# A mixture-of-experts kernel: the second expert's first weights split earlier, the third expert's rows turned later, one set of small loads moved back

## The chip, the cores and the metric

The kernel runs on one core of a Trainium2 chip. Its five engines work from instruction streams of their own: TensorE (PE, with its weight loads shown apart as PEld), VectorE (DVE), ScalarE (ACT), GpSimd (POOL) and SyncE (SP), which here issues nearly all loads. The metric is the device time of one execution in microseconds (us), median of the runs. Before the change it is 405.98 us (3 runs, 405.19 to 406.72).

## The reference

Two parts, one feeding the other. The first is a recurrent attention over 4 batches, 8 heads, 768 steps and 48 channels per head; the second is a mixture of 8 experts over its 3072 rows of 384 columns, where each row goes to the one expert with the highest logit:

```
y[:, :, t] = einsum('bhd,bhde->bhe', rt, state + u*kt (x) vt)
state      = wt * state + kt (x) vt
logits = x @ w_gate;  expert_idx = argmax(logits);  gate_w = softmax(logits)[expert_idx]
for e in range(8):                       # rows sorted by expert
    h = maximum(x_sorted[lo:hi] @ w1[e], 0.0)      # 384 -> 1024
    y_sorted[lo:hi] = h @ w2[e]                    # 1024 -> 384
out = gate_w[:, None] * y_sorted[inv_perm]
```

Everything is float32, and the experts' products must keep float32's accuracy.

## The kernel before

The attention part and the routing take the first 186 us; the routed rows are scattered into a DRAM buffer `xs`, each expert having a region, with two extra columns, the gate weight and the row's number (the "tag"). What the change touches is the part behind it, the function `moe`, which runs the eight experts one after the other, e = 0 to 7 (e is the place in this order; e = 1 is "the second expert").

**Splitting.** TensorE multiplies in a reduced float32 format, so each operand is split in two: a high part H, written by ScalarE (`ACT.Copy` into the reduced type), and a low part L = value - H, written by VectorE. A product is three matmuls: H by H, H by L and L by H. What is split: the weights of an expert in four groups (g = 0 and 1 the halves of w1, g = 2 and 3 the halves of w2; `W[e][2](g)`, lines 1076 and 1078, results `w1H`, `w1L`, `w2H`, `w2L`), the rows (`xsplit`, lines 1247 and 1248, `xH` and `xL`, in three column pieces c = 0 to 2), and the hidden layer (`hH`, line 1282, and `hL`, line 1283).

**One expert on TensorE.** `mm1(e, f)` for f = 0 to 7 makes 128 of the 1024 hidden columns each, nine matmuls into one of four PSUM banks in turn (`ps`, `pt`, `pp`, `pw`), which hH and hL then read. So mm1 of f + 4 needs the bank that hL of f frees. Then the second product, for d = 0 to 2, 24 matmuls each (three for every f), into the banks `pk` and `py`: `mm2` (turned: the result has the 384 output columns on partitions, and `yturn` turns it back by VectorE) for experts with more than 384 places for rows, `mm2d` for the first expert, with 256, and the last ones. The second expert has 464 columns of rows.

**Order of the work.** All is issued in the order in which the code is written (`tc.manual_schedule()`): each engine works through its own list in that order, and waits by semaphores for what others write. So where `xturn`, `xsplit` and the weight splits stand among the `mm1` calls sets what ScalarE and VectorE do between the hidden columns. Two tables say where the next expert's rows are turned and split: `turn(e, t)` is called after each f (t = f) and after each d (t = 8 + d), and does `xturn` (line 1240, one VectorE transposition of the gathered rows `xg` into `xT`) where the first number of the tuple stands and the three `xsplit` where the others do:

```
XF = ((7,7,8,8),(2,3,4,5))
for j, at in enumerate(XF[e > 0]):
    if at == t:
        if j: xsplit(e + 1, j - 1)
        else: xturn(e + 1)
```

**Loads.** SP issues, per expert and in this order: weight halves into four staging buffers `wstage` (line 1057; a buffer is free when its former group has been split), zeros behind the next expert's rows (line 1107), the gathered rows `xg` of the next expert (line 1230, one buffer, rows of 384 B) and the tags (line 1217, elements of 8 B). A DMA that touches `xs` waits for the ones before it that wrote there.

Of the kernel before, what the change touches and what calls it, by code (L numbers as in the profile page):

```python
# [27 lines left out]
FILL = ((0, 0, 0, 0), 0, 2, 0, 1, 5, 8, 0, 0, (99, 99, 20, 0), (0, 2, 0, 0), (0, 0, 0, 0))  # L28
TAIL = (1, 1, 1, 1)
XV = (1, 3)  # L30
XF = ((7,7,8,8),(2,3,4,5))
EA = (4, 5, 6, 7)
TP = 2
PULSE = (3, 2, 1)
# [12 lines left out]
def wkv_moe(ctx: ExitStack, tc: tile.TileContext, r, k, v, w, u, w_gate, w1, w2, out):  # L47
# [21 lines left out]
    NR = NT + TOPB * TB + P  # L69
# [964 lines left out]
    def turned(e):  # L1034
        return CAPS[e - 1] > 3 * P if e else (CAP - EARLY) % P > 0
# [55 lines left out]
    W = {0: weights(0)}  # L1091
    X = {}
# [5 lines left out]
    def following(e):  # L1098
        at = {}
        for nm, t, lo, hi in (("src", perm, 1, E - 1), ("end", ends, NR, E * NR - 4 * zp - P)):  # L1100
            at[nm] = nc.values_load(t[0:1, e:e + 1], engines=(mybir.EngineType.SP,), min_val=lo, max_val=hi)
        X["src", e + 1] = at["src"]
        W[e + 1] = weights(e + 1, at["src"])
        return at["end"]

    def zero_rows(end):
        nc.sync.dma_start(xs[ds(end, 4 * zp)].rearrange("(q p) x -> p q x", p=zp),
                          zrow[:zp, None, :].to_broadcast([zp, 4, ROW]))
# [88 lines left out]
    def moe():  # L1197
        with ExitStack() as a:
# [4 lines left out]
            def span(e):  # L1203
                return (EARLY, CAP) if e == 0 else (0, CAPS[e - 1])

            def blocks(e):
                lo, hi = span(e)
                return [(q, min(P, hi - q)) for q in range(lo, hi, P)]

            def tags(e, at):  # L1210
                lo, hi = span(e)
                n = hi - lo
                tag = X["tag", e] = tp.tile([P, TOPB, 2], F32, name="tag")
                if turned(e):
                    nq = -(-n // TB)
                    for g in range(P // TB):
                        nc.sync.dma_start(tag[g * TB:(g + 1) * TB, :nq], xs[ds(at, nq * TB), DM:DM + 2]
                                          .rearrange("(q t) x -> t q x", t=TB))
                    return
                nf = n // P  # L1220
                nc.sync.dma_start(tag[:, :nf], xs[ds(at, nf * P), DM:DM + 2].rearrange("(q t) x -> t q x", t=P))
                if n % P:
                    nc.sync.dma_start(tag[:n % P, nf], xs[ds(at + nf * P, n % P), DM:DM + 2])

            def xload_(e, src):
                n = CAPS[e - 1]
                nq = -(-n // TB)
                xg = X["g", e] = rp.tile([P, TOPB, XG], F32, name="xg")[:, :nq]
                for g in range(P // TB):
                    nc.sync.dma_start(xg[g * TB:(g + 1) * TB], xs[ds(src * NR, nq * TB), g * XG:(g + 1) * XG]  # L1230
                                      .rearrange("(q t) x -> t q x", t=TB))
# [5 lines left out]
            def xturn(e):  # L1237
                xg = X["g", e]
                X["T", e] = rp.tile([P, TOPB, XG], F32, name="xT")[:, :xg.shape[1]]
                nc.vector.transpose(X["T", e].rearrange("p q (c t) -> p q c t", c=KD),  # L1240
                                    xg.rearrange("p q (t c) -> p q c t", c=KD))
                xalloc(e)

            def xsplit(e, c):
                src = X["T", e][:, :, c * TB:(c + 1) * TB]
                hh, ll = (X[nm, e][:, c, :src.shape[1] * TB].rearrange("p (q t) -> p q t", t=TB) for nm in "HL")
                nc.scalar.activation(hh, src, AF.Copy)
                nc.vector.tensor_tensor(ll, src, hh.bitcast(F32), op=OP.subtract)
# [19 lines left out]
            def mm1(e, f):  # L1268
                ws = W[e][0]
                lo, hi = span(e)  # L1270
                n = hi - lo
                p = bank(("ps", "pt", "pp", "pw")[f % 4])[:, :n]
                sl = slice(f * P, (f + 1) * P)
                terms = [(c, x, y) for c in range(KD) for x, y in ("HH", "HL", "LH")]
                if f == 0:
                    terms.sort(key=lambda t: t[2] == "L")
                for j, (c, x, y) in enumerate(terms):
                    nc.tensor.matmul(p, ws["1" + x][:, c, sl], X[y, e][:, c, :n],  # L1278
                                     start=(j == 0), stop=(j == len(terms) - 1))
                hh = hp.tile([P, TOP], F32R, name=f"hH{f}")[:, :n]  # L1280
                hl = hp.tile([P, TOP], F32R, name=f"hL{f}")[:, :n]
                nc.scalar.activation(hh, p, AF.Relu)
                nc.vector.scalar_tensor_tensor(hl, p, 0.0, hh.bitcast(F32), op0=OP.max, op1=OP.subtract)  # L1283
                X["h", e, f] = (hh, hl)
# [47 lines left out]
            def yscat(e, q):  # L1332
                nc.gpsimd.memset(spacer, 0.0)
                d = nc.gpsimd.indirect_dma_start(  # L1334
                    out=out.rearrange("n (g x) -> (n g) x", g=XP),
                    out_offset=bass.IndirectOffsetOnAxis(ap=X["i", e][:, q:q + 1], axis=0),
                    in_=X["o", e][:, q], in_offset=None, bounds_check=XP * NT - 1, oob_is_err=False)
                for s in oscat:
                    tc.declare_no_dep(d.ins, s.ins, reason="every token has a row of its own")
                oscat.append(d)  # L1340
# [15 lines left out]
                otail(o, n, tag[:, 1:2])  # L1356

            def turn(e, t):
                for j, at in enumerate(XF[e > 0]):
                    if at == t:  # L1360
                        if j:
                            xsplit(e + 1, j - 1)
                        else:
                            xturn(e + 1)
# [8 lines left out]
            for e in range(E):  # L1373
                nx = e + 1 < E
                if nx:
                    if e == 0:
                        tags(0, EARLY)
                        zero_rows(res["end"])
                    elif e > 1:
                        zero_rows(following(e))  # L1380
                    W[e + 1][3](wres)
                    if e:
                        xload_(e + 1, X["src", e + 1])
                        tags(e + 1, X["src", e + 1] * NR)
                        for g in range(4):
                            W[e + 1][1](g)
                    else:
                        W[1][1](0)
                        xload_(1, X["src", 1])
                        W[1][1](1)  # L1390
                        zero_rows(following(1))
                        W[1][1](2)
                        W[1][1](3)
                        tags(1, X["src", 1] * NR)
                for f in range(KF):
                    mm1(e, f)
                    if e > 0 and turned(e - 1):
                        left = X["left"]
                        for _ in range(-(-len(left) // (KF - f))):
                            yscat(e - 1, left.pop(0))  # L1400
                    if e == 0 and f == 5:
                        places()
                    if (e, f) == VF[0]:
                        outcome(yp)
                    if (e, f) == VF[1]:
                        verdict(yp)
                    for at, g, which in late.get(e, ()):
                        if at == f:
                            W[e][2](g, which)
                    if nx:  # L1410
                        turn(e, f)
                if nx:
                    W[e + 1][2](0)
                else:
                    nc.gpsimd.drain()
                for d in range(KD):
                    if turned(e):
                        mm2(e, d)
                        yturn(e, d)
                    elif d < len(blocks(e)):  # L1420
                        mm2d(e, d)
                    if nx:
                        turn(e, KF + d)
                        if e or d == 0:
                            W[e + 1][2](d + 1)
                if turned(e):
                    lo, hi = span(e)
                    X["left"] = list(range(-(-(hi - lo) // TB)))

    moe()  # L1430
    mstk.close()

# [135 lines left out]
```

## Time and profile before

| | us |
|---|---|
| median of 3 runs | 405.98 |
| the profiled execution | 406.11 |
| its span, first to last instruction | 404.3 |
| TensorE busy | 380.5 (94%) |
| VectorE busy | 293.1 (72%) |
| POOL busy | 238.5 (59%) |
| ScalarE busy | 213.5 (53%) |
| first expert on TensorE, from its first matmul to the second expert's | 188.16 to 205.15 |
| second expert, the same | 205.15 to 238.37 |

The profile is of one execution; 1.8 us of its time lie outside its span. The granted TensorE clock is 0.996 of full speed on the mean, and full in every stretch that is read below. A busy share of 94% says little by itself: the ends of matmuls are modelled. What TensorE loses is read from the starts of its matmuls and from the list of its waits.

### The profile page before, as it was taken

What the parts mean: (1) busy time and instruction counts of PE and PEld (TensorE: products, weight loads), DVE (VectorE), ACT (ScalarE), POOL (GpSimd) and SP (SyncE); (2) the same over time, 40 slices, a digit from 0 to 9 for tenths busy, and PEclk for the clock granted to TensorE, in tenths of its full rate; (3) what the DMA queues carried; (4) which work ended last, traced back from release to release, by engine and by line L of the source; (5) the groups of instructions that cost most, each with busy time, mean ns of one, the idle gap of its engine ahead of it and who ended that gap; (6) DMA issues with size and microseconds to landing.
All of it is one profiled execution on the core that took longest, in us unless ns stands there. A gap on an engine that the chain in (4) does not pass through costs nothing.

```text
span 404.3 us, 13751 instructions
## 1 busy us (share of the span) xinstructions
PE 380.5 (94%) x5546; PEld 338.2 (84%) x5547; DVE 293.1 (72%) x498; ACT 213.5 (53%) x439; POOL 238.5 (59%) x469
## 2 busy tenths in 40 slices
PE   8879999999989989999999999999999999999992
PEld 4567777787767768789988799999999999999992
DVE  7688998888888876567776968787596695864510
ACT  6667668656755764454264564465455554471300
POOL 8655777669976994762120008848748488388211
PEclk9999999999999999999999999999999999999998
DMA  9999998668775954236999769757847576521001
GB/s 141 170 166 157 166 188 179 131 126 174 173 150 123 267 157 147 104 111 192 230 237 212 241 124 357 170 167 209 227 152 183 178 244 175 179 98 37 35 19 40
DMA packets 149039, 66.10 MB, mean 163 GB/s; under 512 B 127774, under 2 KB 140283, under 8 KB 148966
## 3 DMA queue, kind: packets, MB, share of 16 engines
q1 hardware_dynamic: 143030, 55.36, 59.5%
q0 software_dynamic: 4336, 9.47, 6.7%
q8 instruction: 45, 0.74, 0.8%
q10 hardware_dynamic: 1600, 0.30, 0.5%
q14 instruction: 28, 0.23, 0.2%
HBM read 49.72 MB, written 15.87 MB: 162 GB/s over the span
## 4 chain that ended last, share of the span: by engine, by line
PE 64%; DVE 10%; SPq 6%; DMA 6%; POOL 5%; issue 4%; ACT 4%; POOLq 0%; DVEq 0%; ACTq 0%
PE ps L1278 5%; PE pt L1278 5%; PE pk L1265 5%; PE pk L1266 5%; PE pw L1278 5%; PE pp L1278 5%; PE pk L1264 5%; SPq L417 4%; PE both L528 3%; DMA xg<-xs 3%; PE py L596 3%; PE py L1266 3%; PE py L1265 3%; PE py L1264 3%; DVE TT L567 2%
## 5 line engine op out<-in xcount | busy, mean ns | idle before, releaser
L1334 POOL DMA_INDIRECT out_dram<-yo,yi x68 | 85.9, 1264 | 69.4 <-DVE yo L1330 54.7
L1078 DVE TENSOR_TENSOR w2L<-wstage,w2H 128x1536 fp32r<-128x1536 f32 x16 | 33.0, 2060 | 9.1 <-ACT w2H L1076 9.1
L519 POOL TENSOR_TENSOR SC<-eye,qT 128x384 f32<-128x384 f32 x32 | 26.5, 828 | 15.9 <-ACT qT L512 15.6
L278 POOL DMA_INDIRECT xs<-xr,slu x24 | 29.0, 1207 | 8.7 <-DVE slu L272 4.3
L444 POOL TENSOR_TENSOR rk<-rT,kT 112x384 f32<-112x384 f32 x32 | 31.9, 996 | 1.9 <-ACT rT L465 1.9
L1078 DVE TENSOR_TENSOR w1L<-wstage,w1H 128x1536 fp32r<-128x1536 f32 x16 | 28.0, 1756 | 6.8 <-ACT w1H L1076 6.5
L474 DVE TENSOR_TENSOR_SCAN L<-pw,stepb 112x390 f32<-112x390 f32 x30 | 28.7, 956 | 4.6 <-PE pw L453 2.1
L1076 ACT ACTIVATE w2H<-wstage 128x1536 fp32r<-128x1536 f32 x16 | 31.5, 1977 | 0.0
L497 POOL TENSOR_TENSOR Kd<-kT,L 112x384 f32<-112x384 f32 x32 | 29.8, 932 | 1.5 <-ACT kT L469 1.5
L482 DVE TENSOR_TENSOR_SCAN F<-pw,bfw 112x390 f32<-112x390 f32 x30 | 29.0, 968 | 0.9
L516 ACT ACTIVATE Kt<-both 128x288 f32<-128x288 f32 x32 | 13.1, 410 | 31.2 <-PE both L528 30.1
L528 PE MATMUL both<-RF,Kd 48*64 48x112 f32 x768 | 27.9, 262 | 1.6 <-issue 1.6
L1265 PE MATMUL pk<-hL,w2H 128*128 128x464 f32 (+4 forms) x80 | 28.6, 357 | 0.6 <-DVE hL L1283 0.6
L1266 PE MATMUL pk<-hH,w2L 128*128 128x464 f32 (+4 forms) x80 | 28.5, 356 | 0.0
L1264 PE MATMUL pk<-hH,w2H 128*128 128x464 f32 (+4 forms) x80 | 28.4, 355 | 0.0
L532 DVE COPY_PREDICATED SC<-mask,both 128x384 f32<-128x384 uint32 x32 | 19.0, 593 | 11.4 <-POOL SC L519 5.4
L1084 POOL DMA_INDIRECT out_dram<-orow,tag x8 | 9.3, 1160 | 26.8 <-DVE orow L1355 26.3
L567 DVE TENSOR_TENSOR_SCAN TT<-PT,AT 112x576 f32<-112x576 f32 x16 | 22.8, 1425 | 1.2 <-ACT PT L562 1.2
L546 PEld LDWEIGHTS py<-V,Kt 64*48 64x48 f32 x704 | 17.1, 121 | 7.6 <-ACT qT L512 4.8
L1076 ACT ACTIVATE w1H<-wstage 128x1536 fp32r<-128x1536 f32 x16 | 23.5, 1478 | 0.0
L528 PEld LDWEIGHTS both<-RF,Kd 48*64 48x64 f32 x768 | 21.4, 134 | 2.0 <-issue 2.0
L546 PE MATMUL py<-V,Kt 64*48 64x48 f32 x704 | 22.2, 212 | 0.7 <-ACT Kt L516 0.4
(307 smaller groups left out, 1180.5 us busy)
## 6 DMA issues: line engine op xcount, KB each, us to landing
wstage<-in_moe_w_dram SPq DMA_DIRECT2D x28, 768.0 KB
xs<-zrow SPq DMA_DIRECT2D x7, 723.8 KB
in_w<-in_w_dram SPq DMA_DIRECT2D x30, 144.0 KB
in_k<-in_k_dram SPq DMA_DIRECT2D x30, 144.0 KB
in_r<-in_r_dram SPq DMA_DIRECT2D x30, 144.0 KB
V<-in_v_dram SPq DMA_DIRECT2D x15, 168.0 KB
V<-in_v_dram SPq DMA_DIRECT2D x16, 144.0 KB
xg<-xs SPq DMA_DIRECT2D x12, 156.0 KB
```

The costliest lines, as they stand in the source:

```text
L444: nc.gpsimd.tensor_tensor(t[:GP], T["rT", i][:GP], T["kT", i][:GP], op=OP.mult)
L497: nc.gpsimd.tensor_tensor(KDM[i % 3][:GP], chunks(T["kT", i][:GP], C), T["L", i][:, :, 1:], op=OP.mult)
L528: nc.tensor.matmul(psS[half(side, c % 2), side, c // 2, :], KDM[i % 3][kr, c, :], RF[i % 6][kr, c, :], start=True, stop=True)
L546: nc.tensor.matmul(p[64 * side:64 * side + D, par, q, :], T["Kt", i][ts, side, q, :], vat(un, side, par, h * NB + q), start=fresh, stop=fresh)
L567: nc.vector.tensor_tensor_scan(t[:GP].rearrange("p e c -> p (e c)"), PT[un % 2][:GP].rearrange("p e c -> p (e c)"), AT[un % 3][:GP].rearra ...
L1076: nc.scalar.activation(hh, sv, AF.Copy)
L1078: nc.vector.tensor_tensor(ll, sv, hh.bitcast(F32), op=OP.subtract)
L1264: nc.tensor.matmul(p, lh, rh, start=first, stop=False)
L1265: nc.tensor.matmul(p, lh, rl, start=False, stop=False)
L1266: nc.tensor.matmul(p, ll, rh, start=False, stop=last)
L1278: nc.tensor.matmul(p, ws["1" + x][:, c, sl], X[y, e][:, c, :n], start=(j == 0), stop=(j == len(terms) - 1))
L1334: d = nc.gpsimd.indirect_dma_start(out=out.rearrange("n (g x) -> (n g) x", g=XP), out_offset=bass.IndirectOffsetOnAxis(ap=X["i", e][:, q:q ...
```

## The change

Three edits, all around the first and the second expert (e = 0 and e = 1).

```
-XF = ((7,7,8,8),(2,3,4,5))
+XF = ((7,7,8,8),(5,6,7,8),(2,3,4,5))
...
-                for j, at in enumerate(XF[e > 0]):
+                for j, at in enumerate(XF[min(e, 2)]):
...
                     if e:
                         xload_(e + 1, X["src", e + 1])
-                        tags(e + 1, X["src", e + 1] * NR)
+                        for k in range(1 if e == 1 else e + 1, e + 2):
+                            tags(k, X["src", k] * NR)
...
                         W[1][1](3)
-                        tags(1, X["src", 1] * NR)
...
+                    if (e, f) == (0, 6):
+                        W[1][2](0)
                     if nx:
                         turn(e, f)
                 if nx:
-                    W[e + 1][2](0)
+                    if e:
+                        W[e + 1][2](0)
```

First, the split of the second expert's first half of w1 moves from behind the first expert's hidden columns to between its f = 6 and f = 7, ahead of the transposition of the second expert's rows. Second, during e = 1 the third expert's rows are turned after f = 5 and not after f = 2, and split after f = 6, f = 7 and d = 0. Third, the second expert's tag loads go to the place behind the third expert's rows. No instruction is added or taken away.

On ScalarE, from the first expert's last hidden columns to the second expert's first (numbers in the names tell buffers apart). Before:

```order
L1282 ACTIVATE hH_4471<-pp 128x256
L1282 ACTIVATE hH_4485<-pw 128x256
L1247 ACTIVATE xH<-xT 128x480
L1076 ACTIVATE w1H<-wstage 128x3x512
L1247 ACTIVATE xH<-xT 128x480 x2
L1076 ACTIVATE w1H<-wstage 128x3x512
L1282 ACTIVATE hH_4597<-ps 128x464
```

On the same engine in the same place, changed:

```order
L1282 ACTIVATE hH_4466<-pp 128x256
L1076 ACTIVATE w1H<-wstage 128x3x512
L1282 ACTIVATE hH_4482<-pw 128x256
L1247 ACTIVATE xH<-xT 128x480 x3
L1076 ACTIVATE w1H<-wstage 128x3x512
L1282 ACTIVATE hH_4597<-ps 128x464
```

The first `w1H` now stands ahead of the last `hH` (f = 7, bank `pw`), which on VectorE is followed in the same way: `w1L` stands ahead of the last `hL`.

On VectorE, the second expert's hidden columns from f = 2 on (bank `pp`) to the first weights of the third expert. Before:

```order
L1283 SCALAR_TENSOR_TENSOR hL_4628<-pp,hH_4627 128x464
L1240 STREAM_TRANSPOSE xT<-xg 128x1344
L1283 SCALAR_TENSOR_TENSOR hL_4646<-pw,hH_4645 128x464
L1248 TENSOR_TENSOR xL<-xT,xH 128x448
L1283 SCALAR_TENSOR_TENSOR hL_4662<-ps,hH_4661 128x464
L1078 TENSOR_TENSOR w2L<-wstage,w2H 128x1536
L1248 TENSOR_TENSOR xL<-xT,xH 128x448
L1283 SCALAR_TENSOR_TENSOR hL_4680<-pt,hH_4679 128x464
L1248 TENSOR_TENSOR xL<-xT,xH 128x448
L1283 SCALAR_TENSOR_TENSOR hL_4696<-pp,hH_4695 128x464
L1283 SCALAR_TENSOR_TENSOR hL_4710<-pw,hH_4709 128x464
```

Changed:

```order
L1283 SCALAR_TENSOR_TENSOR hL_4628<-pp,hH_4627 128x464
L1283 SCALAR_TENSOR_TENSOR hL_4642<-pw,hH_4641 128x464
L1283 SCALAR_TENSOR_TENSOR hL_4656<-ps,hH_4655 128x464
L1078 TENSOR_TENSOR w2L<-wstage,w2H 128x1536
L1283 SCALAR_TENSOR_TENSOR hL_4672<-pt,hH_4671 128x464
L1240 STREAM_TRANSPOSE xT<-xg 128x1344
L1283 SCALAR_TENSOR_TENSOR hL_4690<-pp,hH_4689 128x464
L1248 TENSOR_TENSOR xL<-xT,xH 128x448
L1283 SCALAR_TENSOR_TENSOR hL_4706<-pw,hH_4705 128x464
L1248 TENSOR_TENSOR xL<-xT,xH 128x448
```

The transposition moved from behind the third `hL` (f = 2) to behind the sixth (f = 5); one of the three `xL` falls behind the last `hL` and one into the second product.

On SP the four loads of `xg` for the third expert's rows and the four of `tag` for the second expert's change places, behind the second expert's last two weight loads; the rest of SP's list keeps its order, and so does TensorE's whole list.

## Rows read from the trace of the kernel before

**Rows 1.** The page, busy time of TensorE (us, share, instructions).

```profile
PE 380.5 (94%) x5546; PEld 338.2 (84%) x5547; DVE 293.1 (72%) x498; ACT 213.5 (53%) x439; POOL 238.5 (59%) x469
```

**Rows 2.** Waits of TensorE, 180 to 404 us: us in total, times, longest.

```profile
PE pw L1278 <- DVE hL L1283: 0.7, 1, 0.7
PE pk L1265 <- DVE hL L1283: 0.6, 2, 0.4
...
PE ps L1278 <- DVE w1L L1078: 0.3, 1, 0.3
```

**Rows 3.** Timeline of TensorE, second expert: start us, us, what [idle before <-releaser].

```profile
205.15 0.37 PE L1278 MATMUL ps<-xH,w1H 128*128 128x464 f32 x1
205.79 0.48 PE L1278 MATMUL ps<-xH,w1L 128*128 128x464 f32 x1 [0.26 <-DVE w1L L1078]
...
207.76 0.38 PE L1278 MATMUL pt<-xH,w1H 128*128 128x464 f32 x1
...
217.19 0.38 PE L1278 MATMUL pp<-xH,w1H 128*128 128x464 f32 x1
...
219.99 0.48 PE L1278 MATMUL pw<-xH,w1H 128*128 128x464 f32 x1 [0.75 <-DVE hL L1283]
...
221.97 0.37 PE L1264 MATMUL pk<-hH,w2H 128*128 128x464 f32 x1
...
228.30 0.37 PE L1264 MATMUL py<-hH,w2H 128*128 128x464 f32 x1
...
233.33 0.37 PE L1264 MATMUL pk<-hH,w2H 128*128 128x464 f32 x1
...
238.37 0.36 PE L1278 MATMUL ps<-xH,w1H 128*128 128x436 f32 x1
```

**Rows 4.** Timeline of VectorE, 196 to 225 us.

```profile
199.79 2.14 DVE L1240 STREAM_TRANSPOSE xT<-xg 128x1440 f32<-128x1440 f32 x1 [1.99 <-DMA xg<-xs]
...
203.97 1.76 DVE L1078 TENSOR_TENSOR w1L<-wstage,w1H 128x1536 fp32r<-128x1536 f32 x1 [0.72 <-ACT w1H L1076]
...
217.43 1.98 DVE L1240 STREAM_TRANSPOSE xT<-xg 128x1344 f32<-128x1344 f32 x1 [1.98 <-DMA xg<-xs]
219.33 0.60 DVE L1283 SCALAR_TENSOR_TENSOR hL<-pw,hH 128x464 fp32r<-128x464 f32 x1
220.05 0.62 DVE L1248 TENSOR_TENSOR xL<-xT,xH 128x448 fp32r<-128x448 f32 x1
...
222.66 2.27 DVE L1078 TENSOR_TENSOR w2L<-wstage,w2H 128x1536 fp32r<-128x1536 f32 x1 [1.43 <-ACT w2H L1076]
```

**Rows 5.** Timeline of ScalarE, 195 to 223 us.

```profile
195.94 0.38 ACT L1282 ACTIVATE hH<-pp 128x256 fp32r<-128x256 f32 x1 [0.68 <-PE pp L1278]
...
202.47 1.47 ACT L1076 ACTIVATE w1H<-wstage 128x1536 fp32r<-128x1536 f32 x1
...
208.02 0.56 ACT L1282 ACTIVATE hH<-ps 128x464 fp32r<-128x464 f32 x1 [1.72 <-PE ps L1278]
...
219.44 0.58 ACT L1247 ACTIVATE xH<-xT 128x448 fp32r<-128x448 f32 x1 [5.20 <-DVE xT L1240]
219.93 0.54 ACT L1282 ACTIVATE hH<-ps 128x464 fp32r<-128x464 f32 x1
220.36 2.26 ACT L1076 ACTIVATE w2H<-wstage 128x1536 fp32r<-128x1536 f32 x1
```

**Rows 6.** Timeline of TensorE, first expert: its first matmul that reads the last hL.

```profile
200.78 0.33 PE L1266 MATMUL pk<-w2H,hL 128*128 128x384 f32 x1
```

**Rows 7.** Timeline of SP: issue of the second expert's first weights.

```profile
186.42 0.64 SPq L1057 DMA_DIRECT2D wstage<-in_moe_w_dram  x1
```

**Rows 8.** The page, DMA issues: count and KB each.

```profile
wstage<-in_moe_w_dram SPq DMA_DIRECT2D x28, 768.0 KB
xs<-zrow SPq DMA_DIRECT2D x7, 723.8 KB
```

**Rows 9.** Busy time by stretch: length, engines (instructions), PEclk, DMA share, GB/s.

```profile
185.74:193.00 7.26, 6.94 (x57) 6.30 (x56) 5.51 (x10) 4.01 (x8) 3.23 (x5) 1.00 0.91 254
```

## The prediction, made before the changed kernel was run

> **What bounds the kernel now.** Three views, in this order. The page first: TensorE is busy 94% of the span [rows 1]. Busy ends of matmuls are modelled, so the share only says where to look. Then the list of TensorE's waits over the experts: hardly 2 us in all, and the ones with a price are in the second expert, on `hL` and on `w1L`, both written by VectorE [rows 2]. Behind the second expert nothing is listed up to the end of the span, so from there to the end TensorE sets the time, and a microsecond that the second expert gets back should reach the end. Third, the timeline of TensorE, because a wait in the list counts only the idle part: a matmul behind a stall also takes longer itself (0.48 us where others take 0.37 [rows 3]). What the stalls cost is read from start to start.
>
> Clean pace: from f = 1 to f = 6 nothing stalls, 207.76 to 217.19, five steps, 1.886 us for each hidden column block of nine matmuls; the second and third d take 5.03 and 5.04 us for 24 matmuls [rows 3]. By that pace the second expert takes 8 x 1.886 + 3 x 5.035 = 30.2 us. It takes 238.37 - 205.15 = 33.2 us. The 3.0 us between them lie in three places [rows 3]:
> - f = 0: 207.76 - 205.15 = 2.61, 0.72 over the pace. Its second matmul waits for `w1L`.
> - before f = 7: f = 6 starts at 217.19, so f = 7 was due at 219.08 and starts at 219.99, 0.91 late, and takes 0.09 over the pace itself: 1.00. It waits for `hL` of f = 3, which frees bank `pw`.
> - d = 0: 228.30 - 221.97 = 6.33, 1.30 over the pace. Two matmuls wait for `hL` again [rows 2].
>
> The causes stand on VectorE and ScalarE. `w1L` started at 203.97 only, behind a `w1H` at 202.47, itself behind the row transposition at 199.79 which had waited for its gather [rows 4, 5]. And the third expert's transposition stands behind the third `hL`: VectorE sat idle 1.98 us for the gather `xg` until 217.43, then transposed 1.98 us, and `hL` of f = 3 came at 219.33. ScalarE meanwhile sat idle 5.20 us before `xH`, with `hH` of f = 4 queued behind it until 219.93 and `w2H` until 220.36; `w2L` until 222.66 [rows 4, 5]. That backlog is what d = 0 pays for.
>
> **The first split moved.** The price is in the first expert: ScalarE now does `w1H` between `hH` of f = 6 and of f = 7, VectorE `w1L` ahead of the last `hL`. `hH` of f = 6 ends at 195.94 + 0.38 = 196.32; `w1H` 1.47 gives 197.79; `w1L` 1.76 gives 199.55; the last `hL` at most 0.60 (its row is one of 464 columns, here there are 256) gives 200.15 [rows 4, 5]. TensorE reads that `hL` first at 200.78 [rows 6]. Cover 0.63 us, price nothing. If the cover is gone, TensorE waits as long as `hL` is late, one for one.
>
> Behind it on VectorE stands the transposition of the second expert's rows: from 199.79 to at worst 200.15, 0.36 later, so `xT` is there at 202.29. Three `xH` of 0.58 bring ScalarE to 204.03 [rows 5] and TensorE wants the first at 205.15, as before. VectorE then has `xL`, the first output scaling and two `xL`, four pieces of about 0.62 behind the first `xH`: 202.87 + 2.48 = 205.35 [rows 4], against the seventh matmul of f = 0, due at 205.15 + 6 x 0.21 = 206.41. `w1L` is long there. So f = 0 runs at the pace: **0.72 gained.**
>
> Is the half of w1 in SBUF at 196.32? The trace has no row for its landing. It ran without waiting at 202.47 [rows 5], which bounds it from above. It was issued at 186.42 [rows 7], behind 724 KB of zeros issued just before: 1492 KB with its own 768 [rows 8], some 1.53 million bytes. From 185.74 to 193.00 the engines moved 254 GB/s x 7.26 us = 1.84 million [rows 9]. I estimate a landing near 193, three us before it is wanted. For this edit I take nothing lost, and 202.47 for the far end, below.
>
> The Trainium skill speaks against such an estimate: "DMA: Bandwidth & Descriptors", section "Queues, rings and completion order", says that each DMA engine consumes one queue's descriptors in ring order, but that completion is not FIFO per issuing engine, as the engines finish independently. By it the slowest of 16 engines decides and my sum over all says less. The nearest row is the mean itself, and no row here shows single engines; that rule gives the slower rival its place.
>
> **The transposition moved.** With the clean start, f starts at 205.15 + 1.886 f: f = 5 at 214.58, f = 7 at 218.35, d = 0 at 220.24. No transposition stands before `hL` of f = 3 now, so bank `pw` is free in time and f = 7 is not held: **1.00 gained.** What is late next is the row of work behind f = 4. `hH` starts 0.26 after the next block's first matmul (208.02 against 207.76 [rows 3, 5]), so `hH` of f = 4 at 214.84. In a row, without their overlaps: `hH` 0.54 gives 215.38, `w2H` 2.26 gives 217.64, `w2L` 2.27 gives 219.91, `hL` of f = 5 0.60 gives 220.51, the transposition 1.98 gives 222.49 [rows 4, 5]. The gather it needs was there at 217.43 even when it was issued behind the tags, so VectorE has no wait there. Then the first `xH` 0.58 beside `hL` of f = 6 at 223.09, `xL` 0.62 gives 223.71, and the last `hL` 224.31 [rows 4, 5]. TensorE wants `hL` of f = 5 at 220.24 + 16 x 0.21 = 223.60 (there since 220.51), of f = 6 at 224.23 (there since 223.09), of f = 7 at 224.86. The cover of the last is 0.55 us. So d = 0 runs at the pace too: **1.30 gained**, and this is the tightest of the sums.
>
> The second part of the rows' split and the third expert's `w1` fall into d = 0 and d = 1. All of it (two `xL`, two `w1L`, 4.8 us) is done by about 232, and the third expert starts at 205.15 + 30.2 = 235.35.
>
> **The tags moved.** The second expert's tags are first used by the index computation behind its d = 0, whose last matmul came just before 228.30 [rows 3]; their four loads now go out behind the four gathers for the third expert, which before had landed by 217.43 with the tags ahead of them [rows 4]. So some 10 us of cover: price nothing. SP's queue keeps its length, since two groups of four change places; the third expert's weight loads, behind both, go out when they did. By itself this edit gains nothing, as the later transposition no longer waits for `xg`.
>
> **The sum.** 0.72 + 1.00 + 1.30 = 3.0 us. Against the profiled execution: 406.11 - 3.0 = 403.1. That execution lies 0.13 above the median of the runs shown (405.98), so the prediction is **403.0 us**, 0.74% faster. More than 3.0 is not there to be had, as the first expert shows no stall and the later ones none. About 0.5%, 2.0 us, is what a measurement of this kernel can tell from no change.
>
> **Rivals.**
>
> *Only the two early gaps go.* The row behind f = 4 has eight links and 0.55 us of cover. If it comes 1.85 us later than I add up (semaphores between engines, the second half of w2 landing after 215.38 where it was used at 220.36 before), d = 0 stalls as before, 1.30. Gain 1.72, time 404.3. For it: the small margin, and that my `w2H` is asked for 5 us earlier than any row shows it. Against: I left out the overlaps of neighbours (`w2H` at 220.36 starts before `hH` from 219.93 has ended [rows 5]), each worth about 0.1. Chance 0.12.
>
> *Given back later.* The third expert, ready 3 us earlier, could wait for what comes at its old time: its rows' or weights' splits, fed by loads that SP issues behind the tags. Then 406.0. For it: the loads of three experts share one queue. Against: the buffers they wait for are freed earlier by the same change, and no wait is listed after 228. Chance 0.07.
>
> *Slower: the first weights aren't there.* Mechanism: ScalarE stops at `w1H` with `hH` of f = 7 behind it, VectorE at `w1L` with the last `hL` and the transposition behind it, and TensorE stops in the first expert's second product. It decides from a landing at 196.32 + 0.63 = 196.95 on, and costs a microsecond for each one beyond; over 3.0 us, so from 199.95, the change is a loss. At the far end, 202.47, it costs 5.5 us and the others still gain 3.0: 408.5. For it: ahead of it in the queue are the zeros, with the gather and the second half right behind. Against: the bytes moved. Chance 0.05.
>
> **How the numbers follow.** Forecast 403.0 with 0.76, the partial gain 0.12, given back 0.07, slower 0.05. Around the forecast the runs shown spread by 0.8 either way: its own range is 402.2 to 403.8. To leave out no more than two in ten the range has to reach the partial gain at 404.3 with some of that spread, so 402.1 to 405.0; 408.5 and 406.0 stay outside with 0.12. Faster by over 0.5% (below 403.95): the forecast and a little of the partial gain, 0.77. Within 0.5%: the rest of it and the gain given back, 0.18. Slower: 0.05.
>
> **What would show it.** Right: no TensorE wait on `w1L` at f = 0 and the second expert's first two blocks 1.89 apart; no idle VectorE before the third expert's transposition, which starts near 220.4; f = 7 at 218.4, d = 1 at 225.3, the third expert at 235.3. Wrong: TensorE waiting for `hL` in the first expert's second product, ScalarE idle before the moved `w1H`; a wait on `hL` near 224 to 225; or a third expert that starts at 235 and stalls on `xL`, `w1L` or `w2L`.

## The result, and the profile after

The changed kernel takes 401.90 us (median of 8 runs, 400.70 to 403.02), the kernel before 405.48 in the same comparison (8 runs): ratio 0.9919, 95% interval 0.9901 to 0.9937, so 3.3 us (2.6 to 4.0). The forecast was 3.0 us and 403.0 us. The median lies 0.2 below the stated range of 402.1 to 405.0. But in this comparison the kernel before, too, is 0.5 below the 405.98 on which the forecast stood; the ratio times 405.98 is 402.7, inside the range.

All waits of TensorE that are listed for the changed kernel from 180 us on; those on `hL` and `w1L` [rows 2] are gone, and the one that is left lies ahead of the first expert:

```profile
PE pp L1122 <- DMA xr<-xs: 0.3, 1, 0.3
```

TensorE's timeline through its second expert, against [rows 3]:

```profile
204.07 0.38 PE L1278 MATMUL ps<-xH,w1H 128*128 128x464 f32 x1
...
205.97 0.37 PE L1278 MATMUL pt<-xH,w1H 128*128 128x464 f32 x1
...
217.28 0.37 PE L1278 MATMUL pw<-xH,w1H 128*128 128x464 f32 x1
...
219.16 0.37 PE L1264 MATMUL pk<-hH,w2H 128*128 128x464 f32 x1
...
224.20 0.37 PE L1264 MATMUL py<-hH,w2H 128*128 128x464 f32 x1
...
229.24 0.37 PE L1264 MATMUL pk<-hH,w2H 128*128 128x464 f32 x1
...
234.28 0.36 PE L1278 MATMUL ps<-xH,w1H 128*128 128x436 f32 x1
```

f = 0 takes 1.90 us (2.61 before), f = 7 starts on the pace and takes 1.88 (1.98), d = 0 takes 5.04 (6.33). The second expert takes 30.21 us where it took 33.22: 3.01. All behind it only moved: the time from the third expert's start to the eighth's is 133.53 us in both profiles (234.28 to 367.81, 238.37 to 371.90).

The spans differ by 4.5 us (404.3 and 399.8), not 3.0. The first expert starts at 187.06 and not at 188.16, and 0.4 lies behind the last matmul. The 1.1 at the first expert's start is chance: over all profiles told of here that start, behind code which no kernel changes, lies between 185.83 and 189.28.

ScalarE in the changed kernel, the moved `w1H` and the row of work behind f = 4, against [rows 5]:

```profile
194.86 0.38 ACT L1282 ACTIVATE hH<-pp 128x256 fp32r<-128x256 f32 x1 [0.68 <-PE pp L1278]
195.14 1.48 ACT L1076 ACTIVATE w1H<-wstage 128x1536 fp32r<-128x1536 f32 x1
196.51 0.38 ACT L1282 ACTIVATE hH<-pw 128x256 fp32r<-128x256 f32 x1
...
213.76 0.56 ACT L1282 ACTIVATE hH<-ps 128x464 fp32r<-128x464 f32 x1 [1.32 <-PE ps L1278]
214.22 2.27 ACT L1076 ACTIVATE w2H<-wstage 128x1536 fp32r<-128x1536 f32 x1
```

VectorE in the same stretches, against [rows 4]:

```profile
198.32 0.42 DVE L1283 SCALAR_TENSOR_TENSOR hL<-pw,hH 128x256 fp32r<-128x256 f32 x1
198.75 2.12 DVE L1240 STREAM_TRANSPOSE xT<-xg 128x1440 f32<-128x1440 f32 x1
...
219.23 1.99 DVE L1240 STREAM_TRANSPOSE xT<-xg 128x1344 f32<-128x1344 f32 x1
...
222.41 0.63 DVE L1283 SCALAR_TENSOR_TENSOR hL<-pw,hH 128x464 fp32r<-128x464 f32 x1
```

TensorE's reads for which the two `hL` are due:

```profile
199.70 0.33 PE L1266 MATMUL pk<-w2H,hL 128*128 128x384 f32 x1
...
223.78 0.37 PE L1265 MATMUL pk<-hL,w2H 128*128 128x464 f32 x1
```

The first expert's last `hL` ends at 198.74, 0.96 ahead of its read; the second expert's at 223.04, 0.74 ahead. Neither transposition waits for its gather.

### The profile page after: what moved, and what is told of

It reads as the page before. It is cut to its first block, busy times and chain, and to the rows that moved or that the text cites. A ratio compares the mean times of both kernels' runs of the same rounds, so it can differ in the third digit from the quotient of the medians.

```text
span 399.8 us, 13752 instructions
## 1 busy us (share of the span) xinstructions
PE 379.7 (95%) x5546; PEld 338.7 (85%) x5547; DVE 292.6 (73%) x498; ACT 213.7 (53%) x439; POOL 238.6 (60%) x469
## 4 chain that ended last, share of the span: by engine, by line
PE 78%; DVE 8%; POOL 5%; ACT 4%; issue 2%; DMA 1%; POOLq 0%; DVEq 0%; ACTq 0%
PE ps L1278 6%; PE pp L1278 6%; PE pt L1278 6%; PE pw L1278 6%; PE pk L1264 6%; PE pk L1266 6%; PE pk L1265 6%; PE both L528 3%; PE py L596 3%; PE py L1265 3%; PE py L1264 3%; PE py L1266 3%; PE pk L460 2%; DVE F L482 2%; PE py L546 2%
## 5 line engine op out<-in xcount | busy, mean ns | idle before, releaser
L596 PE MATMUL py<-TT,RF 48*64 48x48 f32 x656 | 22.2, 265 | 0.9 <-ACT xr L626 0.6
```

Source lines behind the costliest of these rows:

```text
L596: nc.tensor.matmul(p[side][64 * par:64 * par + 64, q, :], RF[i % 6][kr, c, :C], T["TT", un][kr, :, h * NCH + c], start=(side, par) not in ...
```

## The experiments

Each kernel's edit is shown against the kernel before or the changed one. "Two experts" is the time on TensorE from the first expert's first matmul to the third's, in the profile; "lag" is from the first expert's first matmul to the transposition of the second expert's rows. The columns f = 0 and d = 0 are the time of these steps of the second expert, from start to start; on the pace they take 1.89 and 5.04. A ratio is to the kernel before on the same chip, with its 95% interval.

| kernel | lag | f = 0 | stall before f = 7 | d = 0 | two experts | ratio |
|---|---|---|---|---|---|---|
| before | 11.63 | 2.61 | 0.9 | 6.33 | 50.21 | |
| before_again | 13.78 | 4.80 | 0 | 5.74 | 52.12 | 0.9999 (0.9979 to 1.0019) |
| only_split | 13.05 | 1.90 | 2.4 | 6.32 | 51.00 | 0.9999 (0.9970 to 1.0028) |
| only_tags | 12.00 | 2.97 | 0 | 6.33 | 49.69 | 0.9971 (0.9951 to 0.9991) |
| only_turn | 12.59 | 3.58 | 0 | 5.02 | 48.81 | 0.9952 (0.9936 to 0.9968) |
| no_split | 12.36 | 3.32 | 0 | 5.01 | 48.59 | 0.9970 (0.9944 to 0.9996) |
| no_turn | 11.82 | 1.91 | 0 | 6.23 | 48.41 | 0.9964 (0.9939 to 0.9989) |
| no_tags | 11.60 | 1.90 | 0 | 5.05 | 47.22 | 0.9915 (0.9895 to 0.9934) |
| changed | 11.69 | 1.90 | 0 | 5.04 | 47.22 | 0.9919 (0.9901 to 0.9937) |
| after_again | 12.51 | 1.91 | 0 | 5.05 | 47.21 | 0.9905 (0.9878 to 0.9931) |
| turn_f3 | 12.89 | 1.90 | 0 | 5.05 | 47.22 | 0.9916 (0.9887 to 0.9944) |
| gather_first | 9.57 | 1.91 | 0 | 5.71 | 47.90 | 0.9939 (0.9913 to 0.9964) |
| gather_first2 | 9.56 | 1.90 | 0 | 5.79 | 47.90 | one run |
| split_f0 | 16.62 | 1.90 | 0 | 5.04 | 54.27 | 1.0120 (1.0101 to 1.0139) |

**only_split**, the first edit alone:

```
+                    if (e, f) == (0, 6):
+                        W[1][2](0)
...
-                    W[e + 1][2](0)
+                    if e:
+                        W[e + 1][2](0)
```

> The kernel before with the first edit alone: the second expert's first half of w1 is split between f = 6 and f = 7 of the first. Theory of the gather: f = 0 takes 1.89 us and not 2.61, but the gather lands when it did, so VectorE only waits longer for it and f = 7 starts when it did; the second expert still takes 33.2 us and the time is the same as before, within 0.3 us. Rival, each edit owns its gap: 0.72 us faster, second expert 32.5 us.

Measured: no change in time, with an interval of 1.2 us either way, in which the rival's 0.72 would fit too. The profile speaks against the rival: f = 0 is clean, f = 7 waits longer, and the second expert takes 34.00 us, not 32.5. It is not the theory's 33.2 either, since the first gather landed later than in the first profile (lag 13.05). VectorE's two transpositions, then TensorE's f = 7 and the third expert's start:

```profile
202.33 2.15 DVE L1240 STREAM_TRANSPOSE xT<-xg 128x1440 f32<-128x1440 f32 x1 [0.93 <-DMA xg<-xs]
...
219.35 1.96 DVE L1240 STREAM_TRANSPOSE xT<-xg 128x1344 f32<-128x1344 f32 x1 [3.16 <-DMA xg<-xs]
```

```profile
221.89 0.48 PE L1278 MATMUL pw<-xH,w1H 128*128 128x464 f32 x1 [2.24 <-DVE hL L1283]
...
240.28 0.36 PE L1278 MATMUL ps<-xH,w1H 128*128 128x436 f32 x1
```

What f = 0 gained VectorE waits away before the second transposition (3.16 us; 1.98 in [rows 4]). The theory of the gather holds: the first edit alone shows no gain.

**no_turn**, the changed kernel with `XF[1]` back at (2,3,4,5):

```
-XF = ((7,7,8,8),(5,6,7,8),(2,3,4,5))
+XF = ((7,7,8,8),(2,3,4,5),(2,3,4,5))
```

> The changed kernel with its second edit undone: the third expert's rows are turned after f = 2 again. Theory of the gather: the stall before f = 7 and in d = 0 came from the gather landing late behind the tags; with the tags behind it, it lands by about 212, before hL of f = 2 is done (213.7), so the transposition waits for nothing and the second expert takes 30.2 to 30.5 us: 2.7 to 3.0 us faster than the kernel before. Rival, each edit owns its gap: the place of the transposition is what cost 2.3 us, so the second expert takes 32.5 us and the kernel is only 0.7 us faster than before.

Measured: between the two, second expert 31.40 us, 1.5 us faster than before (0.4 to 2.5). f = 7 is clean as the theory said, but d = 0 kept 1.19 of its 1.30. VectorE, then ScalarE:

```profile
213.28 1.98 DVE L1240 STREAM_TRANSPOSE xT<-xg 128x1344 f32<-128x1344 f32 x1 [0.88 <-DMA xg<-xs]
...
218.53 2.27 DVE L1078 TENSOR_TENSOR w2L<-wstage,w2H 128x1536 fp32r<-128x1536 f32 x1 [1.45 <-ACT w2H L1076]
```

```profile
215.29 0.58 ACT L1247 ACTIVATE xH<-xT 128x448 fp32r<-128x448 f32 x1 [4.08 <-DVE xT L1240]
215.78 0.54 ACT L1282 ACTIVATE hH<-ps 128x464 fp32r<-128x464 f32 x1
216.22 2.28 ACT L1076 ACTIVATE w2H<-wstage 128x1536 fp32r<-128x1536 f32 x1
```

The gather landed 10.44 us after the second expert's start, which is 214.51 on the clock of the changed kernel's profile, on which I had it by about 212. And `hH` of f = 4 and `w2H` stand in ScalarE's list behind the `xH` that waits for the transposition. In the changed kernel `w2H` started 10.15 us after the second expert's start, here 13.38.

**only_tags**, the third edit alone:

```
-                        tags(e + 1, X["src", e + 1] * NR)
+                        for k in range(1 if e == 1 else e + 1, e + 2):
+                            tags(k, X["src", k] * NR)
...
-                        tags(1, X["src", 1] * NR)
```

> The kernel before with the third edit alone: the second expert's tags are loaded behind the third expert's rows. Theory of the gather: it lands some 4 us earlier, the transposition after f = 2 finds it there, and only the 0.72 us of f = 0 stay with at most 0.3 in d = 0: second expert 30.9 to 31.2 us, 2.0 to 2.3 us faster than before. Rival, each edit owns its gap: nothing waits for tags, so no gain, 33.2 us.

Measured: a gain, 1.2 us (0.4 to 2.0), which the rival excluded, but not the 2.0 expected. The stall before f = 7 is gone, f = 0 and d = 0 keep theirs. In the profile the second expert takes 32.68 us, not the 30.9 to 31.2 expected: the third expert's transposition still waits 1.05 us for its gather.

**before_again**, the kernel before, unedited.

> The kernel before once more, for a second profile. Both theories: second expert 33.2 us, with the same three stalls. If the 1.1 us by which the experts began earlier in the profile of the changed kernel are chance, the start of the first expert (188.16 in the first profile) differs here too by some tenths to one microsecond; if they belong to the change, it is 188.2 again.

Measured: the same time, and the experts begin at 186.43, so the early start was chance. But the stalls aren't the same three: the lag is 13.78 and the first two experts take 1.9 us longer. VectorE's two transpositions, TensorE at the second expert's first matmuls, and the stretches:

```profile
200.21 2.14 DVE L1240 STREAM_TRANSPOSE xT<-xg 128x1440 f32<-128x1440 f32 x1 [4.15 <-DMA xg<-xs]
...
217.59 1.98 DVE L1240 STREAM_TRANSPOSE xT<-xg 128x1344 f32<-128x1344 f32 x1 [0.37 <-DMA xg<-xs]
```

```profile
204.42 0.48 PE L1278 MATMUL ps<-xH,w1H 128*128 128x464 f32 x1 [0.84 <-ACT w1H L1076]
206.21 0.51 PE L1278 MATMUL ps<-xH,w1L 128*128 128x464 f32 x1 [1.31 <-DVE w1L L1078]
```

```profile
203.00:205.00 2.00, 1.06 (x5) 0.45 (x3) 1.26 (x2) 2.00 (x3) 0.00 (x0) 1.00 0.94 244
205.00:207.00 2.00, 0.79 (x3) 0.71 (x4) 2.00 (x3) 1.73 (x2) 0.04 (x1) 0.88 0.93 300
207.00:209.00 2.00, 2.00 (x7) 1.72 (x6) 2.00 (x3) 0.00 (x0) 1.21 (x2) 0.50 1.09 372
...
211.00:213.00 2.00, 2.00 (x11) 1.79 (x11) 0.64 (x1) 1.31 (x2) 0.34 (x2) 1.00 0.61 137
```

The columns are those of [rows 9]. What f = 0 loses over the pace in the kernel before is 0.72 us in one profile and 2.91 in the other.

**no_split**, the changed kernel without the lines shown at only_split.

> The changed kernel with its first edit undone: the first half of w1 is split behind the first expert's hidden columns again. Both theories: w1L comes 0.6 to 0.7 us late for f = 0, f = 0 takes 2.6 us, all else is clean: second expert 30.9 us, 2.3 us faster than the kernel before. Should the wait for w1L push the whole row of work behind it, hL of f = 7 would be late too and d = 0 stall again by some tenths.

Measured: d = 0 is clean, and f = 0 takes 3.32, more than the 2.6 expected. The ratio gives 1.2 us, with an interval from 0.2 to 2.3, whose upper end is the 2.3 forecast; the two medians lie 2.0 apart.

**only_turn**, the second edit alone (`XF[1]` = (5,6,7,8)).

> The kernel before with the second edit alone: the third expert's rows are turned after f = 5. Theory of the gather: only the 0.72 us of f = 0 stay, second expert 30.9 us, 2.3 us faster than before, the same as with the third edit alone to 0.3 us. Rival: the later place alone isn't enough because the gather is still behind the tags, so more than 1 us stays, 31.9 us or more.

Measured: 1.9 us (1.3 to 2.6). The second expert takes 31.83 us, near the rival's 31.9, but not by the rival's cause: f = 7 and d = 0 are clean with the tags in front, and all of the rest is f = 0, which takes 3.58. VectorE's first transposition, then TensorE's wait in f = 0 and the start of f = 1:

```profile
199.58 2.13 DVE L1240 STREAM_TRANSPOSE xT<-xg 128x1440 f32<-128x1440 f32 x1 [2.97 <-DMA xg<-xs]
```

```profile
205.57 0.48 PE L1278 MATMUL ps<-xH,w1L 128*128 128x464 f32 x1 [1.22 <-DVE w1L L1078]
...
207.55 0.38 PE L1278 MATMUL pt<-xH,w1H 128*128 128x464 f32 x1
```

These two, only_tags and the first profile of the kernel before give one rule: f = 0 ends 7.97 to 7.98 us after the transposition starts (199.58 to 207.55, 198.56 to 206.53, 199.47 to 207.45, 199.79 to 207.76), wherever the second expert could have begun.

**no_tags**, the changed kernel without the third edit.

> The changed kernel with its third edit undone: the tags are loaded ahead of the third expert's rows again. Theory of the gather: it lands near 216.3, the transposition is asked for at 219.2, so nothing waits and the second expert takes 30.2 us, 3.0 us faster than before. Rival: the tags in front do cost, VectorE idle before the transposition and 30.5 us or more.

Measured: as the theory had it, second expert 30.21 us, no wait, 3.4 us faster than before (2.7 to 4.3). The third edit shows no gain beside the other two.

**split_f0**, the first split asked for much too early:

```
-                    if (e, f) == (0, 6):
+                    if (e, f) == (0, 0):
```

> The changed kernel with the first half of w1 split behind f = 0 of the first expert, not f = 6. It asks for the weights at about 188.9 on the clock of the changed kernel's profile, far ahead of their estimated landing near 192 (issue 185.3). If the estimate is right ScalarE stands idle some 3 us before w1H, hL of f = 1 follows at about 195.6, f = 5 of the first expert waits for its bank from 192.5 to about 195.7, and the first expert takes 20.2 us where it took 17.0: about 3.2 us slower than the changed kernel. If they land right behind the zeros at 190, about 1.5 us; if near 195, where the changed kernel first asks for them, 6 us.

Measured: the first expert takes 24.06 us where it took 17.01, 7.05 more, beyond all three forecasts. ScalarE, TensorE, and the stretches:

```profile
193.63 1.48 ACT L1076 ACTIVATE w1H<-wstage 128x1536 fp32r<-128x1536 f32 x1 [5.29 <-DMA wstage<-in_moe_w_dram]
```

```profile
197.29 0.58 PE L1278 MATMUL pt<-xH,w1H 128*128 128x256 f32 x1 [5.13 <-DVE hL L1283]
```

```profile
194.00:196.00 2.00, 0.00 (x0) 0.00 (x0) 0.86 (x1) 2.00 (x5) 0.00 (x0) 0.55 1.18 226
...
198.00:200.00 2.00, 2.00 (x11) 2.00 (x11) 1.90 (x3) 0.34 (x1) 0.00 (x0) 0.50 0.59 179
```

The weights, issued at 184.62, land 9.0 us later, not the 6.6 of the prediction (186.42 to 193). f = 5 starts 5.29 us late; f = 5 and f = 6 then take 2.09 and 1.80 for 1.06, with the granted clock at 0.50. So the slower rival's mechanism is real, and here it cost more than one for one.

**turn_f3**, the changed kernel with `XF[1]` = (3,4,5,6).

> The changed kernel with the third expert's rows turned after f = 3 and split after f = 4, 5 and 6. The gather should land as in the run that turned them after f = 2 (10.4 us after the second expert's start), so the transposition starts at the same time as there, some 10.4 us in, after waiting 0 to 0.5 us. Theory of the row: what made d = 0 stall there was that ScalarE's hH of f = 4 and w2H stood behind the xH that waits for the transposition; here both stand ahead of it, so d = 0 takes 5.03 us and the second expert 30.2 us: the same time as the changed kernel within 0.2%. Rival, the late gather: with the transposition at the same time d = 0 stalls as there by about 1.2 us, second expert 31.4 us.

Measured: the second expert takes 30.21 us, though the transposition waited 1.44 us and started 11.57 us in, later than in no_turn (10.44). VectorE, then ScalarE:

```profile
216.93 1.98 DVE L1240 STREAM_TRANSPOSE xT<-xg 128x1344 f32<-128x1344 f32 x1 [1.44 <-DMA xg<-xs]
```

```profile
215.05 0.56 ACT L1282 ACTIVATE hH<-ps 128x464 fp32r<-128x464 f32 x1 [1.32 <-PE ps L1278]
215.50 2.26 ACT L1076 ACTIVATE w2H<-wstage 128x1536 fp32r<-128x1536 f32 x1
218.94 0.58 ACT L1247 ACTIVATE xH<-xT 128x448 fp32r<-128x448 f32 x1 [1.18 <-DVE xT L1240]
```

`w2H` stands ahead of the waiting `xH` now. So what d = 0 paid for was the order of the list, not the gather as such. On VectorE the transposition moved too, behind `hL` of f = 3; but in no_turn VectorE itself waited 1.45 us for `w2H` before `w2L`, so ScalarE's list is the one that counts there.

**after_again**, the changed kernel, unedited.

> The changed kernel once more, for a second profile. Second expert 30.2 us with no wait of TensorE whatever the start of the first expert is, though the gather and the first weights land some tenths to one microsecond elsewhere against it. If the stalls come back where the experts begin early against the loads, then f = 0 is over 1.9 us or the first expert over 17.0 us in it.

Measured: the same 47.21 us, with a lag 0.82 longer than in its first profile. The kernel before passes such a difference on to f = 0; the changed one does not.

**gather_first**, the kernel before with one other change:

```
-                        W[1][1](0)
                         xload_(1, X["src", 1])
+                        W[1][1](0)
                         W[1][1](1)
```

> The kernel before with one other change and none of the three: the gather of the second expert's rows is issued ahead of the first half of its w1, so 768 KB fewer stand before it. Theory that the landing of this gather sets what f = 0 loses (in four profiles f = 0 ended 7.97 us after the transposition started): it lands some 3 us earlier, the transposition starts right behind the first expert's last hL, 9.3 us after the first expert's start and not 11.6 to 13.8, f = 0 takes 1.9 us, and since the next loads follow from it the stall before f = 7 goes too; at most 1.2 us stay in d = 0. Second expert 30.2 to 31.5 us, 2 to 4 us faster than the kernel before. Rival, the place of the split: w1H still stands behind the transposition on ScalarE and its weights are now issued later, so f = 0 still waits for w1L and takes 2.6 us or more.

Measured: 2.5 us faster (1.5 to 3.5). The second expert takes 30.89 us, f = 0 and f = 7 are clean, d = 0 keeps 0.68. The rival falls: `w1H` still stands behind the transposition, and f = 0 loses nothing. VectorE's two transpositions, the first without a wait:

```profile
196.80 2.12 DVE L1240 STREAM_TRANSPOSE xT<-xg 128x1440 f32<-128x1440 f32 x1
...
214.17 1.98 DVE L1240 STREAM_TRANSPOSE xT<-xg 128x1344 f32<-128x1344 f32 x1 [0.35 <-DMA xg<-xs]
```

**gather_first2**, the same again.

> The same kernel once more, for a second profile: the same, with the gather's landing against the first expert's start some tenths elsewhere.

Measured, in one run of 403.07 us: 47.90 us for the two experts again, f = 0 1.90, d = 0 5.79. Nothing tried beats the changed kernel; no_tags and turn_f3 equal it.

## Why the prediction was right, and where it was not

**What bounds the kernel: right.** TensorE's starts gave three places and 3.0 us, and the profile after has exactly these back, f = 0, f = 7 and d = 0 each within 0.03 of the forecast. Nothing new took their place and nothing was given back later: both first rivals are out.

**The three stalls are not three prices.** In all seven profiles that turn the third expert's rows after f = 2 (before, before_again, only_split, only_tags, no_turn, gather_first, gather_first2) that transposition waits for its gather, and the third expert starts 20.93 to 20.97 us after it, whatever f = 0 lost (217.43 to 238.37 in [rows 3, 4], 219.35 to 240.28 in only_split). So there the landing of that one gather sets the end, and f = 0, f = 7 and d = 0 only show where TensorE spends the delay. The gather hangs on the one before it. SP's zeros wait for the second expert's gather (which reads `xs`, where they write), and the tags and then the third expert's gather follow them. SP's waits in the kernel before, 195 to 215 us, and its issues:

```profile
SPq L1107 <- DMA xg<-xs: 3.2, 1, 3.2
SPq L1217 <- DMA xs<-zrow: 2.3, 1, 2.3
```

```profile
199.87 0.42 SPq L1107 DMA_DIRECT2D xs<-zrow  x1
...
205.60 3.35 SPq L1217 DMA_DIRECT2D tag<-xs  x4
209.20 3.72 SPq L1230 DMA_DIRECT2D xg<-xs  x4
```

**"More than 3.0 is not there to be had": wrong by the profiles, and this is the mis-sized term.** The 0.72 of f = 0, and the 3.0 with it, were one draw: they follow mostly from when the second expert's gather lands. The first profile had the shortest lag of the five with that order of split and gather: 11.63; the others 12.00, 12.36 and 12.59 cost f = 0 1.08, 1.43 and 1.69 over the pace, and at 13.78 the first two experts together lost 4.9 against the changed kernel's 47.22. The changed kernel took 47.21 to 47.22 in both profiles. So its gain is 3.0 to 4.9 us by the two profiles of the kernel before. The ratios, 3.3 (2.6 to 4.0) and 3.8 (2.8 to 4.9), lie there, but their intervals also hold 3.0: that the median gain is more than forecast is not shown, nor how often each draw comes.

**The first split, cost nothing: right, for half of the reasons.** I had the weights landing near 193, three us before they were asked for. They land 9.0 us (split_f0) to 10.3 us (only_split, where ScalarE waited 0.34 for them) after issue, which on the clock of the kernel before is 195.4 to 196.7 against 196.32. So there is hardly any cover in the landing. What held was the other one, 0.96 us between the last `hL` and its read: in the six profiles that split behind f = 6 the first expert took 16.99 to 17.01 us. The sum of bytes was the wrong tool, as the stretches from the issue of the zeros to the landing show, in split_f0 and in only_split:

```profile
183.94:193.63 9.69, 7.75 (x61) 6.87 (x59) 4.67 (x7) 3.07 (x6) 4.34 (x12) 1.00 0.98 246
```

```profile
186.82:197.79 10.97, 10.67 (x88) 10.03 (x87) 8.84 (x21) 5.32 (x11) 4.30 (x12) 1.00 0.99 242
```

The engines moved 2.38 and 2.65 million bytes in them, 0.86 and 1.1 more than zeros and weights; the estimate gave these two the whole rate. What the rest was no run shows; the gather behind them in the queue, issued in these stretches, can be most of it (four loads of 180 KB). The sentence of the Trainium skill set against it ("DMA: Bandwidth & Descriptors", section "Queues, rings and completion order": completion is not FIFO per issuing engine) pointed the right way: the measured 9.0 to 10.3 us are later than a sum in order gives, though no run shows single DMA engines. The chance of 0.05 for the slower rival was therefore low: with 0.96 us of cover a landing up to 197.28 is harmless, and the latest seen is 0.6 short of that.

**The later transposition: right.** Forecast at 220.3 to 220.5 on the old clock, it started at 219.23, which is 220.33 on that clock, with the 1.1 added; the last `hL` had 0.74 us of cover for 0.55. turn_f3 shows why it works: `hH` of f = 4 and `w2H` no longer stand behind a wait for a gather. That the gather "as such" was half of the cause, as my theory for no_turn and only_tags had it, fell: the earlier gather saves f = 7, but with the transposition behind f = 2 each microsecond that it starts later counts in d = 0 (0.68 at 9.93 us into the second expert in gather_first, 1.19 at 10.44 in no_turn), up to the 1.30 of the first profile, where f = 7 pays the rest.

**The tags: right beside the second edit,** where they gain nothing (no_tags). Alone they gain 1.2 us (0.4 to 2.0), as they bring the gather forward that sets the end there: the third expert's transposition starts 16.72 us after the second's in only_tags and 15.63 in no_turn, and 17.02 to 17.64 after it in the five profiles that turn at the same place with the tags ahead.

**The edits don't add up.** Alone they are worth 0, 1.9 and 1.2 us by their ratios. Taken out of the changed kernel one at a time they cost the two experts 1.37, 1.19 and 0 us in the profile. The first shows a clear gain only beside the second (48.81 us in only_turn, 47.22 in no_tags), since without that a clean f = 0 only lengthens the wait for the next gather; beside the third the ratios give 1.5 against 1.2 us, which is no difference that the intervals show. In these profiles the first and second alone carry the whole gain (no_tags).

## What to carry to other kernels

Before trusting a stall's size, ask what it waits for: a stall that ends with a DMA is one draw of a spread, and moving work so that nothing needed soon stands behind the DMA wins what the draw would have cost, not the size in one profile. In a list worked through in order, look at what is queued behind the waiting instruction; here it was a weight split of 2.3 us, which ran 3.2 us earlier where it did not stand behind the wait. And do not read a landing from bytes moved: bound it by an instruction that waited for it.

## What the runs showed of the hardware that was not expected

- The kernel before paid for its stall twice in one of its two profiles. In before_again TensorE was busy 1.06 and 0.79 us of two stretches of 2 us, and then the granted clock was 0.50, the 1.2 GHz level, in the next; the 464-column matmuls came 0.38 to 0.39 us apart, not 0.21, and f = 0 ended 9.01 us after the transposition started where the four others had 7.97 or 7.98. In split_f0, after 5.1 us without a matmul, the 256-column ones came 0.21 apart, not 0.12, until 200.9. In only_split the wait of 2.24 us left the granted clock at 1.00, also in the stretch with the wait:

```profile
220.00:222.00 2.00, 0.11 (x1) 0.11 (x2) 1.88 (x3) 0.65 (x2) 0.00 (x0) 1.00 0.96 348
```

- A load of 768 KB took 9.0 to 10.3 us from issue to use, with 724 KB of zeros ahead of it and a gather and another such load issued behind it.
